# GpSimd's order at the start of an attention + MoE kernel: first value casts ahead of the band loads, last pair's keys and queries behind the first band table

## The chip, the cores and the metric

The kernel runs on one core of a Trainium2 chip. The time is in device microseconds; before the change it is 389.29 us, the median of 8 runs (388.36 to 390.95).

## What is computed

```python
# attention with a relative position bias; q, k, v: (8, 8, 576, 64)
scores = q @ k.T / 8 + bias_table[bucket(|i - j|)]   # one table column per head
attn   = exp(scores - max) / (sum + 1e-9)
x      = (attn @ v), heads side by side              # (4608, 512)
# act_snake layer
h   = x @ w_in                                       # w_in (512, 2048)
s   = sin(alpha * h)
g   = h + s * s / (alpha + 1e-9)
out = g @ w_out                                      # w_out (2048, 512)
```

The bucket of a distance is constant from a certain distance on. The kernel therefore multiplies exp(scores) by exp(bias - bias of the far bucket), and only in a band of 384 columns around the diagonal; outside it the factor is 1.

## The kernel before

The outer loop runs over the 8 batches. Within a batch the heads are taken in 4 pairs. For each pair TensorE makes scores for four key chunks of 128 keys (one half of the array per head), then a corner product `"t"` for the last 64 keys of both heads, then a last one for the last 64 queries (`plan_qk`, line 648). ScalarE takes the exponential of each (line 742), VectorE multiplies the band (lines 767 and 750, from the tables `m2r` and `mhr`), TensorE multiplies by the values (`plan_av`, line 779), VectorE divides by the sums (lines 839 and 840), and the result is turned into `xT`, the input of the MoE layer.

Keys and queries must be transposed (head dimension on partitions). For batches 0 and 1 TensorE does it: `plan_tr` (line 568) issues 12 transposes per pair and side (line 591), and a copy at line 564 brings them to `kT` or `qT`. Batch 0's first pair comes by SP's queue; the other three are loaded by GpSimd's queue into `nat1`, which shares its memory with a `u` buffer and is shown as `u` in the profile. For pairs 2 and 3 the last 64 keys are copied to `kt` by SP's queue (line 387). From batch 2 on the keys and queries are staged in DRAM and transposed by DMA.

The values of batch 0 come by SP's queue in fp32 (lines 501 and 504) into memory that later holds `w_out`, and GpSimd casts them to fp16: four chunks (line 418) and two halves for the last keys (line 421).

The band tables come from the small bias table: it is loaded by ScalarE's queue (`tabN`, `tabL`), a difference (line 511), an exponential (line 512), a matmul with a constant (line 529), a copy (line 530), a write to DRAM (`e_dram`, line 531). Then GpSimd loads shifted views of that row: `m2r` for heads 0 and 1, `mhr` in two loads, and `m2r` for heads 2 to 7 (lines 466 and 473). GpSimd's instructions run in the order in which they are written: a cast or a load that waits holds back all behind it, the loads of the weights and of batch 1's data too.

From `plan_qk` on, the order of instructions on TensorE, ScalarE and VectorE comes from a planner that runs when the kernel is built (`Plan.run`, line 109). Each task has an estimated length, dependences, a priority and an earliest due time. At each step the planner takes the task that could start first on its engine, and among those within 0.02 us of it the one of the lowest priority number. The engines then follow that order on the chip; the planned times themselves are not used there, only the semaphores are. Where TensorE would stand idle for more than 0.5 planned us before 30, the planner puts in a filler matmul on zeros (`warm`, line 454). Things that the planner can't see, such as loads, stand in constants of due times: `T_PAIR` (keys and queries of pairs 1, 2 and 3), `T_M2` (band multiplies of pair 0, and of the others), `T_MH` (the same for `mhr`), `T_V` (value products of batch 0 and of batch 1).

Of the kernel before, what the change touches and what calls it, by code (L numbers as in the profile page):

```python
# [180 lines left out]
T_FREE = {"PE": 6.8, "ACT": 7.5, "DVE": 7.75}  # L181
T_KT0 = 6.7
T_QT0 = 7.75
T_PAIR = ((6.8, 7.5), (10.0, 12.0), (10.0, 12.0))
T_M2 = (16.8, 20.0)
T_MH = (18.0, 18.0)
T_V = (18.5, 50.0)
T_TR1 = (36.0, 38.5)
T_KQ2 = 50.0
D_SPLIT = 3.5  # L190
# [23 lines left out]
def kernel(  # L214
# [12 lines left out]
    T, H, S, D = q.shape  # L227
# [81 lines left out]
    nat1 = ubs[2][0:SN, 0 : 2 * (H - 2) * SI * D].rearrange("s (kq h x) -> s kq h x", kq=2, h=H - 2)  # L309
# [105 lines left out]
    def cast_v(t, eng, cs):  # L415
        for c in cs:
            if c < 4:
                eng.tensor_copy(out=vs[t][:, c, :, 0:D], in_=vst[t][:, c])
                continue
            z = c - 4  # L420
            eng.tensor_copy(
                out=vhs[t][64 * z : 64 * z + 64, :, VC * z : VC * z + D],
                in_=vhst[t][64 * z : 64 * z + 64],
            )

    def load_nat(dst, h0, h1, src, eng):

        eng.dma_start(out=dst, in_=src[h0:h1].rearrange("h (p i) d -> p h (i d)", i=SI))

    def load_w_in16(js):  # L430
        src = moe_w_in.rearrange("(j p) ff -> p j ff", p=128)
        for j in js:
            nc.gpsimd.dma_start(out=w_in16[:, j, :], in_=src[:, j, :])
# [8 lines left out]
    def clear(eng, i):  # L442
        eng.memset(kts[i][0:64, :, 64:128], 0.0)
        eng.memset(kts[i][64:128, :, 0:64], 0.0)
        eng.memset(vhs[i][0:64, :, VC : 2 * VC], 0.0)
        eng.memset(vhs[i][64:128, :, 0:VC], 0.0)
        eng.memset(vhs[i][0:64, :, D : D + 1], 1.0)
        eng.memset(vhs[i][64:128, :, VC + D : VC + D + 1], 1.0)
        eng.memset(vs[i][:, :, :, D : D + 1], 1.0)
# [14 lines left out]
    def load_m2r(eng, h0, h1):  # L464

        eng.dma_start(
            out=m2r[:, h0:h1],
            in_=bass.AP(tensor=e_dram, offset=EW * h0, ap=[[1, 128], [EW, h1 - h0], [1, XW]]),
        )

    def load_mhr(eng):
        for z in range(2):
            eng.dma_start(
                out=mhr[64 * z : 64 * z + 64],
                in_=bass.AP(tensor=e_dram, offset=EW * z + 192,
                            ap=[[1, 64], [2 * EW, NP], [1, 192]]),
            )

    P_ = nc.gpsimd
# [23 lines left out]
    for z in range(2):  # L503
        nc.sync.dma_start(out=vhst[0][64 * z : 64 * z + 64], in_=vq[z, 512:S])
    for kq, src in ((0, k), (1, q)):
        load_nat(nat1[:, kq, 2:6], 4, H, src[0], P_)

    nc.vector.memset(zz, 0.0)
    clear(nc.vector, 0)
# [6 lines left out]
    def turn0(kq):  # L516
        c = bank("moE").bitcast(F16)
        for i in range(SI):
            nc.tensor.transpose(
                out=c[:, i * SN : i * SN + SN], in_=natb[:, kq, i], identity=id_sb[0:SN, 0:SN]  # L520
            )
        nc.vector.tensor_copy(  # L522
            out=(qTs if kq else kTs)[0][:, 0, :].rearrange("d (p i) -> d p i", i=SI),
            in_=c[:, 0:S].rearrange("d (i p) -> d p i", i=SI),
        )
# [5 lines left out]
    nc.scalar.dma_start(out=e_dram.ap(), in_=e_sb)  # L531
    turn0(1)
    clear(P_, 1)
    load_m2r(P_, 0, 2)
    load_mhr(P_)
    cast_v(0, P_, (0, 1))
    load_m2r(P_, 2, H)
    load_w_in16((0,))
    cast_v(0, P_, (2, 3, 4, 5))
    load_w_in16((1, 2, 3))  # L540
    for kq, src in ((0, k), (1, q)):
        load_nat(nat2[:, kq], 0, H, src[1], P_)
# [185 lines left out]
    def plan_ex(t, y, sc, b, u, ub, m, gate, base, done, x0):  # L728
# [17 lines left out]
        if i == "t":  # L746

            def bh(e):
# [4 lines left out]
            done[(1, 4)] = plan.add({"DVE": 0.19}, bh, [x], base + 10,  # L753
                                     nb=0.0 if t else T_MH[p > 0], use=[ub])
            return x
        w = 0 if i < 4 else 1
        q0, n = QW[w]
        for cc in [i] if i < 4 else range(4):
# [5 lines left out]
            def bd(e, cc=cc, lo=lo, hi=hi):  # L764
# [7 lines left out]
            done[(w, cc)] = plan.add({"DVE": 0.1 + (hi - lo) / 960.0}, bd, [x], base + 10,  # L772
                                     nb=0.0 if t else T_M2[p > 0], use=[ub])
        return x
# [4 lines left out]
    def plan_av(t, p, w, u, ub, done):  # L779
# [15 lines left out]
        if split:  # L795

            def part(e):
                av.v = bank(ab.tag)
                for i, qc in enumerate(QC[w]):
                    for z in range(2):  # L800
                        for c in range(3):
# [3 lines left out]

            prev = [plan.add({"PE": 0.62}, part, us[:3], base + AV_PRI, nb=T_V[t], new=[ab],
                             use=[ub])]
        for i, qc in enumerate(QC[w]):
# [14 lines left out]
            if t == 0 and w == 1 and i == 0:  # L823
                needs = [done[(0, c)] for c in range(4)] + [done[(1, 4)]]
            prev = [plan.add({"PE": 0.12 if split else 0.31}, mm, needs + prev,
                             base + AV_PRI + i, nb=T_V[t] if t < 2 else 0.0,
                             new=[ab] if i == 0 and not split else [],
# [174 lines left out]
    for t in range(T):  # L1002
# [23 lines left out]
        for p in range(NP):  # L1026
            if t == 0 and p + 1 < NP:
                for kq in range(2):
                    tr[(0, p + 1, kq)] = plan_tr(0, p + 1, kq, 100 * (16 * p + 8), T_PAIR[p][kq])
            deps.append(pe_gate + (tr[(t, p, 0)][0] + tr[(t, p, 1)][0] if t < 2 else []))  # L1030
# [69 lines left out]
```

The softmax here doesn't subtract the row's maximum and nothing guards it: scores larger than these inputs give would overflow.

## Time and profile before

| | us |
|---|---|
| median of 8 runs | 389.29 |
| the profiled execution | 390.05 |
| its span, first to last instruction | 388.3 |
| TensorE (PE) busy | 373.5 (96%) |
| ScalarE (ACT) busy | 319.2 (82%) |
| VectorE (DVE) busy | 264.8 (68%) |
| GpSimd (POOL) busy | 82.7 (21%) |
| exponentials of batch 0, first start to last end | 10.61 to 32.93 |
| first sine of the MoE layer | 38.12 |
| first exponential of batch 1 | 56.65 |

In the views of the trace, PE stands for TensorE's matmuls, PEld for its weight loads, ACT for ScalarE, DVE for VectorE, POOL for GpSimd, SP for SyncE. L418 is line 418 of the kernel. A row of the view in order of time has the start, the length, the engine, the line, the operation, output and input, the count of instructions merged in the row and, in brackets, how long the engine was idle before it and what ended that. A length may reach into the next instruction, since instructions are pipelined. A DMA is said to land when its semaphore shows it complete; its time to landing is counted from the start of its issue.

### The profile page before, as it was taken

The page shows a single profiled execution, that of the slowest core. Times are in us where ns is not written, and L with a number is a line of the kernel's source. Part 1 is how long each engine was busy: PE and PEld are TensorE (multiplying, and loading weights), DVE is VectorE, ACT ScalarE, POOL GpSimd, SP SyncE. Part 2 cuts the span into 40 slices and gives each one's busy share as a digit, 9 for nine tenths or more (in the row PEclk, how much of TensorE's full clock was granted, in tenths as well). Part 3 has the DMA queues.
Part 4 walks back from the last instruction along what each step waited for, and adds up shares of the span by engine and source line. Part 5 has one row for each costly group of instructions (what it writes and reads, how often), then busy time and mean ns, then how long its engine had stood idle before and what let it go on. Part 6 is the DMA issues. An engine that isn't in the chain of part 4 may idle for free.

```text
span 388.3 us, 8540 instructions
## 1 busy us (share of the span) xinstructions
PE 373.5 (96%) x3398; PEld 186.6 (48%) x3398; DVE 264.8 (68%) x589; ACT 319.2 (82%) x449; POOL 82.7 (21%) x98
## 2 busy tenths in 40 slices
PE   5989979999999999999999999999999999999996
PEld 2456434555545644555445535543555444444443
DVE  3776986686887698679867977697668718429100
ACT  2896999999999999999999999999999728529210
POOL 6583835072540071006300400000000000000000
PEclk9999999999999999999999999999999999999999
DMA  9899999999999999959991938210021010020122
GB/s 174 180 201 214 176 191 172 149 166 150 170 147 157 189 120 142 182 62 75 146 179 47 71 35 209 61 31 29 29 60 31 29 65 16 30 81 0 56 81 81
DMA packets 151207, 42.55 MB, mean 110 GB/s; under 512 B 140216, under 2 KB 145680, under 8 KB 151168
## 3 DMA queue, kind: packets, MB, share of 16 engines
q0 software_dynamic: 89872, 19.04, 58.8%
q1 hardware_dynamic: 61136, 22.93, 31.8%
q8 instruction: 26, 0.43, 0.5%
q14 instruction: 13, 0.11, 0.1%
q10 hardware_dynamic: 160, 0.04, 0.1%
HBM read 37.73 MB, written 16.52 MB: 140 GB/s over the span
## 4 chain that ended last, share of the span: by engine, by line
PE 88%; ACT 6%; DVE 2%; issue 2%; DMA 1%; ACTq 0%; DVEq 0%
PE sc L452 41%; PE am L452 38%; PE ca L452 4%; PE cb L452 4%; ACT u L742 3%; DMA tabL<-in_bias_table_dram 1%; ACT s L920 1%; DVE g L934 1%; ACT sq L927 1%; PE cb L591 0%; DVE qT L564 0%; PE am L591 0%; DVE qT L522 0%; ACT kT L562 0%; ACT outs L562 0%
## 5 line engine op out<-in xcount | busy, mean ns | idle before, releaser
L742 ACT ACTIVATE u<-sc 128x1024 f16<-128x1024 f32 (+1 forms) x192 | 156.3, 898 | 8.6 <-PE sc L452 7.3
L452 PE MATMUL sc<-xT,w_in 128*128 128x512 f16 x576 | 133.4, 379 | 0.4 <-DVE g L934 0.4
L934 DVE SCALAR_TENSOR_TENSOR g<-sq,inv_a,sc 128x512 f16<-128x512 f16 x144 | 103.8, 745 | 26.1 <-PE am L452 21.4
L452 PE MATMUL am<-w_out,g 128*128 128x512 f16 (+1 forms) x464 | 117.3, 374 | 0.7 <-ACT outs L562 0.7
L920 ACT ACTIVATE s<-sc,alphaT 128x512 f16<-128x512 f32 x144 | 92.4, 680 | 6.5 <-PE sc L452 5.5
L767 DVE TENSOR_TENSOR u<-u,m2r 128x512 f16<-128x512 f16 (+2 forms) x160 | 67.8, 441 | 29.0 <-ACT u L742 27.5
L452 PEld LDWEIGHTS <-g 128*128 128x128 f16 x592 | 54.3, 98 | 66.2 <-issue 14.0
L452 PEld LDWEIGHTS <-w_in 128*128 128x128 f16 x576 | 54.6, 98 | 63.0 <-issue 0.8
L452 PEld LDWEIGHTS <-u 128*128 128x128 f16 x1440 | 54.7, 97 | 16.0 <-issue 4.6
L452 PE MATMUL am<-v,u 128*128 128x65 f16 x1216 | 52.4, 193 | 0.0
L452 PE MATMUL sc<-qT,kT 64*128 64x64 f16 (+1 forms) x512 | 48.3, 295 | 4.1 <-ACT u L742 2.1
L927 ACT ACTIVATE sq<-s 128x512 f16<-128x512 f16 x76 | 47.4, 631 | 2.3 <-DVE g L934 0.5
L398 POOL DMA_DIRECT2D v<-in_v_dram x24 | 21.2, 894 | 109.7 <-PE am L452 107.7
L452 PE MATMUL am<-vh,u 128*128 128x130 f16 x152 | 33.4, 221 | 0.6 <-ACT u L742 0.3
L929 DVE TENSOR_TENSOR sq<-s 128x512 f16<-128x512 f16 x68 | 28.5, 419 | 6.5 <-ACT s L920 6.2
L452 PEld LDWEIGHTS <-kT 64*128 64x128 f16 x512 | 13.8, 95 | 31.8 <-issue 28.9
L840 DVE TENSOR_TENSOR xp<-am,rd 128x384 f16<-128x384 f32 (+1 forms) x56 | 27.5, 491 | 2.1
L839 DVE RECIPROCAL rd<-am 128x6 f32<-128x6 f32 (+1 forms) x60 | 11.2, 187 | 20.0 <-PE am L452 19.6
L562 ACT ACTIVATE outs<-am 128x512 f32<-128x512 f32 x7 | 4.2, 597 | 18.5 <-PE am L452 18.5
L564 DVE COPY outs<-am 128x512 f32<-128x512 f32 (+1 forms) x22 | 14.7, 668 | 3.9 <-PE am L452 3.7
L994 ACT ACT_TABLE_LOAD x13 | 16.7, 1283 | 0.2
L564 DVE COPY outs<-cb 128x384 f32<-128x384 f32 x1 | 0.6, 558 | 23.2 <-PE cb L452 23.2
(92 smaller groups left out, 181.0 us busy)
## 6 DMA issues: line engine op xcount, KB each, us to landing
out_dram<-outs SPq DMA_DIRECT2D x35, 256.0 KB, 2.0
staged_k<-in_k_dram POOLq DMA_DIRECT2D x6, 576.0 KB, 14.5
staged_q<-in_q_dram POOLq DMA_DIRECT2D x6, 576.0 KB, 19.4
v<-in_v_dram POOLq DMA_DIRECT2D x24, 128.0 KB, 8.8
w_in<-in_moe_w_in_dram POOLq DMA_DIRECT2D x4, 512.0 KB, 8.5
w_out<-in_moe_w_out_dram POOLq DMA_DIRECT2D x4, 512.0 KB, 17.3
xT<-xp SPq DMA_TRANSPOSE x72, 3.6
w_out<-in_v_dram SPq DMA_DIRECT2D x4, 256.0 KB, 8.9
```

What stands on the lines that cost most here:

```text
L398: nc.gpsimd.dma_start(out=vs[t % 2][:, c, :, 0:D], in_=vp[128 * c : 128 * c + 128],)
L452: nc.tensor.matmul(out=out, lhsT=lhsT, rhs=rhs, start=start, stop=stop)
L564: k_of(e).tensor_copy(out=o, in_=i)
L742: nc.scalar.activation(out=o, in_=x, func=AF.Exp, scale=0.125)
L767: nc.vector.tensor_tensor(out=io, in0=io, in1=m2[:, 2 * p : 2 * p + 2, x0 : x0 + hi - lo], op=ALU.mult,)
L839: nc.vector.reciprocal(out=r, in_=a[:, :, :, D])
L840: nc.vector.tensor_tensor(out=y.rearrange("p c (z d) -> p c z d", z=2), in0=a[:, :, :, 0:D], in1=r.unsqueeze(3).to_broadcast([128, nq, 2, ...
L920: nc.scalar.activation(out=s16.v, in_=h.v, func=AF.Sin, scale=alphaT[:, f : f + 1])
L927: nc.scalar.activation(out=sq.v, in_=s16.v, func=AF.Square)
L929: k_of(e).tensor_tensor(out=sq.v, in0=s16.v, in1=s16.v, op=ALU.mult)
L934: nc.vector.scalar_tensor_tensor(out=gcell[b].v[:, f, :], in0=sq.v, scalar=inv_a[:, f : f + 1], in1=h.v, op0=ALU.mult, op1=ALU.add,)
L994: nc.scalar.preload_act_table_set(name)
```

## The change

The loads of keys and queries of pairs 2 and 3 (one load each for `k` and `q`) are divided: pair 2's stay where they were, pair 3's are issued by GpSimd later, behind the `mhr` loads. The four casts of value chunks, which stood two between the band loads and two behind the first load of `w_in`, move up: chunks 0 and 1 ahead of the first band load, chunk 2 behind it, chunk 3 behind `mhr`. The two casts of the last keys' values stay. Due times of the planner are changed with it: pair 2's keys and queries earlier (9.5, 10.5), pair 3's later (16.5, 17.5), pair 0's band multiplies earlier (15.9) and the others' later (21.5), `mhr` at 17.8, batch 0's value products later (19.2).

```diff
-T_PAIR = ((6.8, 7.5), (10.0, 12.0), (10.0, 12.0))
-T_M2 = (16.8, 20.0)
-T_MH = (18.0, 18.0)
-T_V = (18.5, 50.0)
+T_PAIR = ((6.8, 7.5), (9.5, 10.5), (16.5, 17.5))
+T_M2 = (15.9, 21.5)
+T_MH = (17.8, 17.8)
+T_V = (19.2, 50.0)
...
     for kq, src in ((0, k), (1, q)):
-        load_nat(nat1[:, kq, 2:6], 4, H, src[0], P_)
+        load_nat(nat1[:, kq, 2:4], 4, 6, src[0], P_)
...
     clear(P_, 1)
+    cast_v(0, P_, (0, 1))
     load_m2r(P_, 0, 2)
+    cast_v(0, P_, (2,))
     load_mhr(P_)
-    cast_v(0, P_, (0, 1))
+    cast_v(0, P_, (3,))
+    for kq, src in ((0, k), (1, q)):
+        load_nat(nat1[:, kq, 4:6], 6, H, src[0], P_)
     load_m2r(P_, 2, H)
     load_w_in16((0,))
-    cast_v(0, P_, (2, 3, 4, 5))
+    cast_v(0, P_, (4, 5))
     load_w_in16((1, 2, 3))
```

## The prediction

> **What bounds the kernel now.** I read the page first (TensorE busy 96% of the span, the chain that ended last 88% TensorE), then the busy times of a few stretches, to see where TensorE is not full:
>
> ```profile
> core 0: us, PE busy (x) PEld busy (x) DVE busy (x) ACT busy (x) POOL busy (x), PEclk, DMA share, GB/s
> 0.00:10.60 10.60, 5.83 (x34) 2.50 (x34) 4.12 (x15) 2.08 (x3) 6.23 (x18) 1.00 0.96 177
> 10.60:33.00 22.40, 21.11 (x282) 11.58 (x283) 17.35 (x46) 20.52 (x25) 14.49 (x21) 1.00 0.98 192
> 33.00:38.10 5.10, 4.75 (x67) 3.21 (x67) 2.77 (x10) 2.37 (x4) 2.53 (x2) 1.00 1.31 222
> 38.10:56.65 18.55, 16.60 (x156) 7.60 (x155) 16.44 (x27) 18.05 (x31) 12.84 (x17) 1.00 1.69 184
> 75.00:100.00 25.00, 25.00 (x348) 14.30 (x347) 17.78 (x51) 23.74 (x32) 9.19 (x8) 1.00 1.89 162
> 200.00:300.00 100.00, 99.60 (x998) 51.03 (x995) 77.51 (x176) 95.89 (x133) 4.79 (x6) 1.00 0.39 67
> ```
>
> From 75 us on TensorE is full, so its remaining work fixes the end. Whatever moves the end of batch 0's attention (about 38 us) moves the end of the kernel by as much: the next stage, to 56.65, has ScalarE at 18.05 of 18.55. The change lies wholly ahead of 38 us. There I read the order in time of GpSimd, ScalarE and VectorE in turn:
>
> ```profile
> 13.64 0.73 POOL L466 DMA_DIRECT2D m2r<-e_dram  x1 [5.70 <-DMA e_dram<-e_sb]
> 14.37 1.26 POOL L473 DMA_DIRECT2D mhr<-e_dram  x2
> 15.62 1.18 POOL L418 CAST v<-w_out 128x512 f16<-128x512 f32 x2
> 16.73 0.84 POOL L466 DMA_DIRECT2D m2r<-e_dram  x1
> ```
>
> GpSimd idles 5.70 us for the bias table (7.94 to 13.64): this is the hole that the change fills.
>
> ```profile
> 14.90 0.65 ACT L742 ACTIVATE u<-sc 128x576 f16<-128x576 f32 x1 [0.19 <-PE sc L452]
> 15.85 8.05 ACT L742 ACTIVATE u<-sc 128x512 f16<-128x512 f32 x9 [0.30 <-PE sc L452]
> 24.39 3.98 ACT L742 ACTIVATE u<-sc 128x1024 f16<-128x1024 f32 x5 [0.48 <-PE sc L452]
> ```
>
> ScalarE's exponentials run from 10.61 to 32.93 with these gaps (0.19, 0.30, 0.48) and two later ones (0.30, 0.15): 1.42 us in all is what a better order on TensorE could give.
>
> ```profile
> 18.25 2.89 DVE L767 TENSOR_TENSOR u<-u,m2r 128x512 f16<-128x512 f16 x4 [0.59 <-DMA m2r<-e_dram]
> 23.45 0.20 DVE L839 RECIPROCAL rd<-am 128x6 f32<-128x6 f32 x1 [1.84 <-PE am L452]
> 24.70 0.41 DVE L767 TENSOR_TENSOR u<-u,m2r 128x512 f16<-128x512 f16 x1
> 35.08 0.20 DVE L839 RECIPROCAL rd<-am 128x6 f32<-128x6 f32 x1 [0.52 <-PE am L452]
> ```
>
> VectorE waits 0.59 us for the first band table, then 1.84 us for pair 0's value product; from 23.45 to 34.56 it has next to no gap. So the first normalisation, that is the place of pair 0's value product on TensorE, sets when batch 0 ends, and the bias table does not.
>
> **The change part by part.** (The planner's due times run ahead of the chip: due 18.5 is met at 22.34 us, due 10 and 12 at 12.42 and 14.79.)
>
> *First casts into the wait.* Two casts, 0.59 us each by the row above. Chunk 0 landed at 9.3 us (issued 2.69, 6.6 to landing), chunk 1 at 13.3 (3.59, 9.7). Were chunk 1 as late again, its cast would end at 13.9 and the first table load, now behind it on GpSimd, would start 0.25 late. But half of the bytes of pairs 2 and 3 leave this stretch: their two loads landed at 11.7 and 13.7, the pair-1 load before them at 8.6, so 576 KB took 5.1 us and half should be through at about 11.2; chunk 1 then lands near 12. The table's own write took until 13.6 (issued 9.17); the quickest landing of any store in the trace is 1.6 us. So the table load starts between 12.6 (chunk 1 cast) and 13.9; I take 12.9. Worth on the path: 0, since it meets VectorE's 0.59 us wait, which is followed by the idle 1.84. If that cover went, VectorE would gain at most the 0.59.
>
> *Later casts.* At 18.12 to 20.82 GpSimd casts while VectorE multiplies; those multiplies take 0.805, 0.957 and 0.745 us against 0.415 and 0.548 after 24.7. Casting two chunks earlier frees up to 1.0 us of VectorE (the excess of these three), again ahead of its idle 1.84: 0.
>
> *Pair 3's transposes leave 13.58 to 17.6.* Each set of 12 costs 0.62 us on the chain, and queries of pair 2 take one of the freed places. So the product before the 0.19 gap is as late as now, while that before the 0.30 gap comes 0.62 earlier: −0.30. Bounds 0 (something else fills the place) and −0.49 (both gaps).
>
> *Pair 3's loads.* GpSimd now has table 0.73, cast 0.59, second table (2 issues) 1.26, cast 0.59, then keys and queries at 0.70 each (the row of the 144 KB loads): keys issued at 12.9+3.17 = 16.1, queries at 16.8. Landing: by the table loads just ahead 3.9 to 4.5 us, so keys at 20.0 to 20.6, queries 20.7 to 21.3; the far bound is the 6.2 us of the second table load, 22.3 and 23.0. (Chunk 2, cast in between at 13.6, landed at 14.6 and chunk 3, cast at 15.5, at 15.4; chunk 2 no earlier than now would hold GpSimd, and so the keys, back 1.0.) Where are they used? Due 16.5 puts the keys behind pair 1's corner product (19.89 now), in the place of the filler matmul at 20.37. TensorE works in order, and behind them is pair 1's last product, whose exponential starts at 21.37 now and at 21.07 after the −0.30. That product needs about 0.45 and the transposes 0.62: keys are wanted by 20.0. At the middle landing, 20.3, TensorE and then ScalarE wait 0.3; queries are a slot later and land in it. +0.3, bounds 0 and +2.3. The Trainium skill (DMA: Bandwidth & Descriptors, Anatomy of one DMA — SWDGE) fits a GpSimd-issued transfer as about 2.0 us plus bytes over 436 GB/s; by it the keys would land 2.3 us after issue and the wait would be 0. The trace's 96 KB loads took 3.9 and 4.2 us from the start of issue, so I keep 0.3.
>
> *The second band table and the values.* The table's second load moves behind the two loads (+1.4), with two casts ahead of it as now, and starts 0.7 earlier: issued near 17.5 instead of 16.73. With its 6.2 us it lands at 23.7 instead of 22.9, or at 25.2 if the queue is full and the 288 KB ahead of it take 1.5 (192 GB/s in the second row above). It is first used at 24.70: hidden by 1.0, or exposed by 0.5. But the due times matter more. Pair 0's value product goes from due 18.5 to 19.2, so it may fall behind one more score product, and each of those waits for an exponential of 1.02 us; pair 1's band multiplies go from due 20.0 to 21.5. The first normalisation (23.45) then shifts by 0 to 1.0; against it, the product in front removes ScalarE's 0.48 gap, which does not help a full VectorE. I take +0.6, bounds 0 and +1.5 (the 1.0 and the exposed table).
>
> *What else is passed.* SP: the two small copies of pair 3's key tail follow its keys, at some 21.5 us plus 4.1 to 7.2 to landing (such copies now), wanted at 30.77. GpSimd: the same instructions follow; the last first-weight load lands at 32.8 and is used at 35.48, batch 1's keys 35.9 and 39.31, the last second-weight quarter 65.1 and 66.33. A queue 1 us later stays under all three: 0.
>
> Sum: −0.30 + 0.3 + 0.6 = +0.6 us. The profiled execution took 390.05 (span 388.3 plus 1.75 around it) and would take 390.65; it stands 0.76 above the median of the eight runs, so against the median 389.29 the forecast is 389.9.
>
> **Rivals.**
> 1. *Late keys (slower).* Pair 3's keys land at 21.2 us or later, the product behind them waits over 1.2 us, ScalarE starves. For it: landings were 6.2 us and more wherever two queues were busy. Against: the queue is at 0.35 to 0.88 busy between 14 and 19 us. Chunk 2 at its old time is enough. Price 1.2 to 2.3 in place of 0.3, with the rest: 390.8 to 391.9.
> 2. *TensorE stays slow (slower).* Up to about 21 us a 512-column filler takes 0.61 and 12 transposes 0.69; later 0.38 (25.70) and 0.45 (39.31), although the granted clock reads 1.00 throughout. The fast rate came only after four fillers in a row (17.33 to 20.37). Pair 3's transposes take the last one's place and may bring a wait. If the fast rate then comes after pair 0's value product (1.61 us, 22.34 to 23.95), that product takes 1.6 longer and VectorE's first normalisation 1.0 to 1.6: 390.7 to 391.5. The Trainium skill (TensorE: Matmul & The Clock Gate, Part 1) says that about 3.4 us of sustained matmuls bring the full clock; by it TensorE, busy since 8.45, would be fast before the fillers and this rival would cost 0. The trace shows over 12 us of busy slow matmuls.
> 3. *The gaps go (faster).* Keys land in time, pair 0's value product is no later, the gaps 0.30 and 0.48 close and VectorE follows (−0.8), up to all 1.42 of gaps and the 0.59 us wait (−2.0): 387.3 to 388.5. For it: VectorE has idle 1.84 us to absorb pair 3's two copies. Against: VectorE is full from 23.45 on.
>
> **How the numbers follow.** Forecast 0.38 (its own range 389.0 to 390.9), rival 1 0.17, rival 2 0.20, rival 3 0.25. Faster or slower means by over 0.3%, 1.2 us, about what a measurement tells from no change. Faster: 0.18 of rival 3 and 0.01 of the forecast. Slower: 0.11 of the forecast, 0.14 and 0.16 of the two slow rivals. The rest, 0.40, is within. The range, 387.8 to 391.9, leaves some 0.2 out: the best third of rival 3 and what lies beyond the prices of rivals 1 and 2.
>
> **What would show it.** Right: GpSimd's wait ahead of the first table load cut to under 1 us (behind the cast of chunk 1); no gap ahead of the exponential at 15.5; a TensorE or ScalarE gap of a few tenths near 20.5; VectorE's first reciprocal near 24.0 and the first sine half a microsecond after 38.1. Rival 1: a wait of the transposes at line 591 on a load, over 1 us. Rival 2: value products of 0.3 to 0.6 us for 9 matmuls near 23. I am wrong if the first reciprocal comes before 23.45, or if the order of the stages after 38 us itself changes TensorE's idle time there.

## The result and the profile after

The changed kernel takes 391.35 us (median of 17 runs, 390.43 to 391.99) against 389.57 us before (46 runs), a ratio of 1.0047 with a 95% interval of 1.0036 to 1.0058: slower by some 1.8 us. The profiled execution took 391.24 us with a span of 389.5.

In order of time, GpSimd (columns: start, length, engine, line, operation, in brackets the idle time before it and what ended it):

```profile
8.92 0.61 POOL L418 CAST v<-w_out 128x512 f16<-128x512 f32 x1 [0.94 <-DMA w_out<-in_v_dram]
11.17 0.62 POOL L418 CAST v<-w_out 128x512 f16<-128x512 f32 x1 [1.64 <-DMA w_out<-in_v_dram]
13.23 0.73 POOL L466 DMA_DIRECT2D m2r<-e_dram  x1 [1.45 <-DMA e_dram<-e_sb]
13.96 0.62 POOL L418 CAST v<-w_out 128x512 f16<-128x512 f32 x1
14.52 1.25 POOL L473 DMA_DIRECT2D mhr<-e_dram  x2
15.76 0.62 POOL L418 CAST v<-w_out 128x512 f16<-128x512 f32 x1
16.32 0.65 POOL L428 DMA_DIRECT2D u<-in_k_dram  x1
16.96 0.64 POOL L428 DMA_DIRECT2D u<-in_q_dram  x1
```

The change does what it says: the wait for the bias table holds two casts and shrinks from 5.70 to 1.45 us. Pair 3's keys are issued at 16.32 and land 3.2 us later, at 19.55. TensorE wanted them a microsecond before:

```profile
17.89 0.69 PE L452 MATMUL sc<-qT,kt 128*128 128x288 f16 x2
19.60 0.45 PE L595 MATMUL cb<-id_sb,u 96*64 96x96 f16 x12 [1.02 <-DMA u<-in_k_dram]
19.98 0.51 PE L452 MATMUL sc<-qT,kT 64*128 64x64 f16 x10
20.41 0.45 PE L595 MATMUL am<-id_sb,u 96*64 96x96 f16 x12
20.96 0.39 PE L452 MATMUL sc<-qT,kT 64*128 64x512 f16 x2
21.87 0.45 PE L452 MATMUL sc<-qT,kT 64*128 64x512 f16 x2 [0.52 <-ACT u L746]
22.26 0.29 PE L452 MATMUL am<-vh,u 128*128 128x130 f16 x1
...
25.11 0.56 PE L452 MATMUL sc<-qT,kT 64*128 64x512 f16 x2
```

The transposes (line 595 now) wait 1.02 us on the load, and the score product behind them waits too. Then the clock falls (busy time by stretch, PEclk is the granted clock):

```profile
core 0: us, PE busy (x) PEld busy (x) DVE busy (x) ACT busy (x) POOL busy (x), PEclk, DMA share, GB/s
18.00:19.00 1.00, 0.58 (x3) 0.05 (x1) 0.91 (x3) 1.00 (x2) 1.00 (x3) 1.00 0.94 132
19.00:20.00 1.00, 0.40 (x14) 0.34 (x16) 0.48 (x2) 0.27 (x1) 0.94 (x4) 1.00 1.21 204
20.00:21.00 1.00, 0.90 (x27) 0.62 (x25) 0.86 (x2) 0.69 (x2) 1.00 (x3) 1.00 1.02 143
21.00:22.00 1.00, 0.48 (x4) 0.15 (x3) 0.66 (x1) 1.00 (x2) 1.00 (x2) 1.00 0.87 246
22.00:23.00 1.00, 1.00 (x14) 0.75 (x13) 0.00 (x0) 1.00 (x2) 1.00 (x2) 0.54 1.10 225
23.00:24.00 1.00, 1.00 (x20) 1.00 (x19) 0.00 (x0) 0.65 (x1) 0.99 (x2) 0.50 0.92 155
24.00:25.00 1.00, 1.00 (x20) 1.00 (x17) 0.75 (x2) 0.00 (x0) 0.28 (x1) 0.50 1.04 201
25.00:26.00 1.00, 1.00 (x11) 0.47 (x9) 0.75 (x3) 0.29 (x1) 0.62 (x1) 0.76 1.11 214
```

From about 22.1 to 25.5 us TensorE runs at half clock. The whole of pair 0's value product lies in this stretch and takes 2.85 us (22.26 to 25.11). In the kernel before it takes 1.61, from the first to the second of these rows:

```profile
22.34 0.23 PE L452 MATMUL am<-vh,u 128*128 128x130 f16 x1
...
23.95 0.60 PE L452 MATMUL sc<-qT,kT 64*128 64x512 f16 x4
```

In the changed kernel ScalarE and VectorE show both losses:

```profile
20.31 3.35 ACT L746 ACTIVATE u<-sc 128x512 f16<-128x512 f32 x4 [1.04 <-PE sc L452]
25.71 3.98 ACT L746 ACTIVATE u<-sc 128x1024 f16<-128x1024 f32 x5 [2.06 <-PE sc L452]
...
24.12 0.20 DVE L843 RECIPROCAL rd<-am 128x6 f32<-128x6 f32 x1 [2.46 <-PE am L452]
25.77 0.41 DVE L771 TENSOR_TENSOR u<-u,m2r 128x512 f16<-128x512 f16 x1
```

ScalarE's gap of 1.04 is the late keys, that of 2.06 (0.48 before) the slow value product. One thing hides part of this when the two profiles are laid side by side: the first exponential starts at 9.14 us here and at 10.61 before, because the bias table landed 4.2 us after its issue and not 5.7. That is no effect of the change. The same instruction took 4.4 to 5.5 us in seven other profiles below, with the loads of pairs 2 and 3 divided or not. So I compare from the first exponential to the first sine of the MoE layer: 27.51 us before, 29.81 after, 2.3 us more. (Four profiles with the order of the kernel before on TensorE give 27.04 to 27.66.) The next stage, to batch 1's first exponential, is 18.53 and 18.29 us. This stretch tells where time is lost; how much is lost at the end is told by the runs, since what follows the first sine varies too: the time of the profiled execution less that of its first sine is 351.6 to 353.4 us in the twelve profiles.

### The profile page after: what moved, and what is told of

It is laid out like the page before. It is cut to its first block, busy times and chain, and to the rows that moved or that the text cites. A ratio compares the mean times of both kernels' runs of the same rounds, so it can differ in the third digit from the quotient of the medians.

```text
span 389.5 us, 8539 instructions
## 1 busy us (share of the span) xinstructions
PE 374.9 (96%) x3396; PEld 187.8 (48%) x3396; DVE 263.9 (68%) x588; ACT 319.2 (82%) x450; POOL 83.1 (21%) x100
## 4 chain that ended last, share of the span: by engine, by line
PE 89%; ACT 4%; DMA 3%; issue 1%; DVE 1%; POOL 1%; ACTq 0%; DVEq 0%
PE sc L452 42%; PE am L452 38%; PE ca L452 4%; PE cb L452 3%; ACT u L746 3%; DMA e_dram<-e_sb 1%; DMA tabL<-in_bias_table_dram 1%; DMA u<-in_k_dram 1%; PE cb L595 0%; ACT s L924 0%; ACT L998 0%; POOL mhr L473 0%; PE am L595 0%; POOL v L418 0%; DVE g L938 0%
## 5 line engine op out<-in xcount | busy, mean ns | idle before, releaser
L771 DVE TENSOR_TENSOR u<-u,m2r 128x512 f16<-128x512 f16 (+2 forms) x160 | 66.5, 433 | 31.9 <-ACT u L746 27.5
L452 PEld LDWEIGHTS <-u 128*128 128x128 f16 x1440 | 56.6, 99 | 15.9 <-issue 4.4
L452 PE MATMUL am<-v,u 128*128 128x65 f16 x1216 | 53.7, 195 | 0.0
```

Of the source, the lines that this page charges most:

```text
L452: nc.tensor.matmul(out=out, lhsT=lhsT, rhs=rhs, start=start, stop=stop)
L771: nc.vector.tensor_tensor(out=io, in0=io, in1=m2[:, 2 * p : 2 * p + 2, x0 : x0 + hi - lo], op=ALU.mult,)
```

## The experiments

Each theory is told in the expectations. The ratio is to runs of the kernel before that were taken along with it; the times (us) are from one profiled execution of each kernel.

| kernel | ratio, 95% interval | first exponential | first sine | between |
|---|---|---|---|---|
| before | 1 | 10.61 | 38.12 | 27.51 |
| the change | 1.0047 (1.0036 to 1.0058) | 9.14 | 38.95 | 29.81 |
| the change, again | 1.0040 (1.0024 to 1.0055) | 10.50 | 40.34 | 29.84 |
| pair 3's loads in the wait | 1.0000 (0.9986 to 1.0015) | 10.39 | 37.74 | 27.35 |
| due times alone | 1.0013 (0.9996 to 1.0030) | 9.36 | 38.57 | 29.21 |
| casts alone | 1.0004 (0.9993 to 1.0016) | 9.62 | 36.66 | 27.04 |
| fillers in the wait | 1.0027 (1.0016 to 1.0038) | 9.38 | 37.86 | 28.48 |
| pair 3 due later | 1.0077 (1.0054 to 1.0100) | 9.31 | 39.26 | 29.95 |
| bias table first | 0.9982 (0.9965 to 0.9998) | 8.75 | 36.41 | 27.66 |
| start freed of the bias table | 0.9964 (0.9947 to 0.9982) | 8.35 | 35.69 | 27.34 |
| fillers at batch 1's start, on before | 0.9992 (0.9976 to 1.0009) | 9.52 | 37.08 | 27.56 |
| the same, on the start freed | 0.9956 (0.9940 to 0.9972) | 8.36 | 35.69 | 27.33 |

**Pair 3's loads in GpSimd's wait.**

```diff
     clear(P_, 1)
+    for kq, src in ((0, k), (1, q)):
+        load_nat(nat1[:, kq, 4:6], 6, H, src[0], P_)
     cast_v(0, P_, (0, 1))
...
     cast_v(0, P_, (3,))
-    for kq, src in ((0, k), (1, q)):
-        load_nat(nat1[:, kq, 4:6], 6, H, src[0], P_)
     load_m2r(P_, 2, H)
```

> The changed kernel with one move: pair 3's two loads are issued by GpSimd in its wait for the bias table, ahead of the first two casts, and not behind mhr. The order on TensorE, ScalarE and VectorE is that of the changed kernel. Theory A (late keys): in the changed kernel TensorE waits 1.02 us for pair 3's keys (landed at 19.55), ScalarE then idles 1.04 and, after a stretch at half clock, 2.06 us; here the keys land by 14 us, the wait is gone and so is most of both gaps: 2 to 3 us under the changed kernel, ratio to the kernel before 0.992 to 0.998. Theory B (the planner's new order costs the time, the wait is hidden): the ratio stays at 1.003 to 1.006 although the wait is gone. Theory C (early bytes): the start of the exponentials, 9.14 us in the changed kernel and 10.61 before, comes from fewer bytes in front of the bias table's loads; it stays at about 9.1 here, since these loads are issued only after the bias table has landed.

Measured: 1.0000 (0.9986 to 1.0015). The whole loss is gone, with every instruction of TensorE, ScalarE and VectorE in the changed kernel's order. The loads go out at 7.99 and 8.62 and nothing waits for them:

```profile
7.99 0.64 POOL L428 DMA_DIRECT2D u<-in_k_dram  x1
...
14.68 0.72 POOL L466 DMA_DIRECT2D m2r<-e_dram  x1 [2.02 <-DMA e_dram<-e_sb]
...
16.08 7.83 ACT L746 ACTIVATE u<-sc 128x1024 f16<-128x1024 f32 x9 [0.21 <-PE sc L452]
24.50 3.98 ACT L746 ACTIVATE u<-sc 128x1024 f16<-128x1024 f32 x5 [0.58 <-PE sc L452]
...
23.57 0.20 DVE L843 RECIPROCAL rd<-am 128x6 f32<-128x6 f32 x1 [1.28 <-PE am L452]
```

ScalarE works through from 16.08, the value product runs at full clock, and the first reciprocal comes 13.18 us after the first exponential (12.84 before, 14.98 in the changed kernel). Theory A holds for the cause. Its size was overrated: I expected 0.992 to 0.998, and got no better than before. The order itself brings no gain. Theory C falls: the exponentials started at 10.39 with the same early bytes as in the changed kernel's profile. The band table went out at 14.68, later than in either kernel, at no cost.

**The due times alone.**

```diff
-T_PAIR = ((6.8, 7.5), (10.0, 12.0), (10.0, 12.0))
-T_M2 = (16.8, 20.0)
-T_MH = (18.0, 18.0)
-T_V = (18.5, 50.0)
+T_PAIR = ((6.8, 7.5), (9.5, 10.5), (16.5, 17.5))
+T_M2 = (15.9, 21.5)
+T_MH = (17.8, 17.8)
+T_V = (19.2, 50.0)
```

> The kernel before with the changed due times alone; loads and casts stand where they stood. Theory A: no load is late, pair 3's keys have landed at 11.7 us and are used at about 20; no wait of the transposes, ratio 0.998 to 1.002. Theory B: the order alone costs it, ratio 1.003 to 1.006. Theory C: exponentials start at 10.6 as before.

Measured: 1.0013 (0.9996 to 1.0030), which decides for neither number alone, but is under what theory B needs for the 1.0047. "No wait of the transposes" was wrong: pair 2's queries are now due earlier and are loaded with pair 3's, 576 KB together, so they land only at 13.3 us:

```profile
13.38 0.69 PE L591 MATMUL cb<-id_sb,u 96*64 96x96 f16 x12 [0.66 <-DMA u<-in_q_dram]
```

Its profile has gaps of 0.46 and 0.91 us on ScalarE for that. The order needs the divided load of pair 2. What remains after dividing it is the run above: nothing.

The same profile shows one thing more. Pair 3's transposes (19.77 and 21.14) waited for no load here, and yet TensorE was still slow: 0.69 us for 12 transposes, and 0.29 for the value product's first matmul. It became fast only near 23.9, within the value product, and ScalarE's gap behind it is 0.98 in place of 0.58 in the run above:

```profile
22.93 0.29 PE L452 MATMUL am<-vh,u 128*128 128x130 f16 x1
...
25.33 3.99 ACT L742 ACTIVATE u<-sc 128x1024 f16<-128x1024 f32 x5 [0.98 <-PE sc L452]
```

So a late load of pair 3 is not the only way to a slow value product.

**The casts alone.**

```diff
     clear(P_, 1)
+    cast_v(0, P_, (0, 1))
     load_m2r(P_, 0, 2)
+    cast_v(0, P_, (2,))
     load_mhr(P_)
-    cast_v(0, P_, (0, 1))
+    cast_v(0, P_, (3,))
     load_m2r(P_, 2, H)
     load_w_in16((0,))
-    cast_v(0, P_, (2, 3, 4, 5))
+    cast_v(0, P_, (4, 5))
```

> The kernel before with the four casts alone moved up (two ahead of the first band load, one behind it, one behind mhr); pairs 2 and 3 are loaded together as before and the due times are the old ones, so the order on TensorE is the old one. Theory A: chunk 1 lands at 13.3 as before, its cast pushes the first band load from 13.64 to about 13.9, VectorE's first band multiply comes 0.3 later in front of an idle 1.84 us; ratio 0.999 to 1.001. If the casts themselves cost (a rival): ratio over 1.003. Theory C: exponentials start at 10.6.

Measured: 1.0004 (0.9993 to 1.0016): the casts cost and bring nothing that these runs can tell from zero. The exponentials started at 9.62 with undivided loads, against theory C once more.

**Fillers in the wait.** Four matmuls on zeros run while TensorE waits for pair 3's keys.

```diff
-            c.v = bank("moE").bitcast(F16)
+            x0 = bank("moE")
+            if (t, p, kq) == (0, 3, 0):
+                for _ in range(4):
+                    full(x0, zz[:, 0:128], zz, True, True)
+            c.v = x0.bitcast(F16)
```

> The changed kernel with four filler matmuls on zeros put ahead of the transposes of pair 3's keys, so that TensorE is busy in most of the time in which it waits for them. Theory A with a clock part: the keys land as late as before and the gap of 1.04 us ahead of pair 1's last exponential stays, but the granted clock does not fall to 0.5 between 22 and 25.5 us and the gap of 2.06 us shrinks to under 1: 1 to 1.5 us under the changed kernel, ratio 1.000 to 1.003. If the half clock is no cause of the lost time: the ratio stays at 1.004 to 1.006.

Measured: 1.0027 (1.0016 to 1.0038). As expected, one loss stays and the other goes:

```profile
15.60 0.65 POOL L428 DMA_DIRECT2D u<-in_k_dram  x1
...
18.62 1.42 PE L452 MATMUL cb<-zz 128*128 128x512 f16 x4
19.98 0.45 PE L599 MATMUL cb<-id_sb,u 96*64 96x96 f16 x12
...
20.69 3.35 ACT L750 ACTIVATE u<-sc 128x512 f16<-128x512 f32 x4 [1.17 <-PE sc L452]
24.61 3.99 ACT L750 ACTIVATE u<-sc 128x1024 f16<-128x1024 f32 x5 [0.58 <-PE sc L452]
```

The gap of 1.04 is 1.17 here, that of 2.06 is 0.58, and the value product takes 1.61 us again (22.57 to 24.18). The fillers change no load and no order of the others, but they hold the transposes too: the keys, issued at 15.60, landed 3.7 us later, at 19.3, while the fillers ran until 19.98, and TensorE has no wait on the load in this profile. Without the fillers the wait would have been some 0.5 us (the product ahead ended at 18.83). So, by the middle values, of the loss of 0.40 to 0.47% some 0.13 to 0.20%, 0.5 to 0.8 us, was the slow clock or more, and 0.27%, 1.05 us, the wait or less. The intervals overlap, so these shares are estimates; that the slow value product cost time, the two gaps show.

**Pair 3 due later**, so that its transposes stand where the load has landed.

```diff
-T_PAIR = ((6.8, 7.5), (9.5, 10.5), (16.5, 17.5))
+T_PAIR = ((6.8, 7.5), (9.5, 10.5), (19.0, 20.0))
```

> The changed kernel with one constant moved: pair 3's keys and queries are due at 19.0 and 20.0 and not at 16.5 and 17.5. Loads and casts are as in the changed kernel, so the keys land as late; their transposes stand behind pair 2's third score product, some 4 us later on TensorE, with two more fillers ahead of them. If the loss is the wait at the place where the transposes stood: no wait on the load, no fall of the granted clock near 22 us, ratio to the kernel before 0.998 to 1.002. If the later loads cost in another way (the second band table or the weights behind them): the ratio stays at 1.003 to 1.006.

Measured: 1.0077 (1.0054 to 1.0100): slower still, and by neither of the two ways. The wait on the load is gone and the value product is fast (1.61 us, 21.99 to 23.60), but the queries' copy now stands deep in VectorE's full stretch:

```profile
28.78 0.42 DVE L844 TENSOR_TENSOR xn<-ca,rd 128x256 f16<-128x256 f32 x1
29.13 0.41 DVE L771 TENSOR_TENSOR u<-u,m2r 128x512 f16<-128x512 f16 x1
29.46 0.75 DVE L568 COPY qT<-am 128x576 f16<-128x576 f16 x1
...
29.10 0.49 ACT L566 ACTIVATE xT<-am 128x384 f16<-128x384 f16 x1 [2.65 <-PE am L881]
31.05 4.81 ACT L746 ACTIVATE u<-sc 128x1024 f16<-128x1024 f32 x6 [1.14 <-PE sc L452]
```

The queries' transposes were done at 24.3, the copy ran at 29.46, and ScalarE, out of scores, idled 2.65 and 1.14 us (and 1.33 ahead of 24.39). In this order the transposes have a window that opens when the load lands and closes when VectorE fills up.

**The change again**, for a second profile.

> The changed kernel once more, unaltered, for a second profile. In the profiles so far the first exponential starts anywhere from 9.1 to 10.6 us, with the landing of the bias table. If an early start is what makes pair 3's keys late (their landing hangs on the queue and not on the start): with a start near 9.2 the wait of the transposes is near 1 us as in the first profile, with a start near 10.5 it is under 0.3. Ratio 1.003 to 1.006.

Measured: 1.0040 (1.0024 to 1.0055), first exponential at 10.50. The wait followed the start, as expected, but not to under 0.3:

```profile
20.42 0.69 PE L595 MATMUL cb<-id_sb,u 96*64 96x96 f16 x12 [0.42 <-DMA u<-in_k_dram]
21.80 0.69 PE L595 MATMUL am<-id_sb,u 96*64 96x96 f16 x12
23.59 0.29 PE L452 MATMUL am<-vh,u 128*128 128x130 f16 x1
...
27.10 3.98 ACT L746 ACTIVATE u<-sc 128x1024 f16<-128x1024 f32 x5 [2.09 <-PE sc L452]
25.45 0.20 DVE L843 RECIPROCAL rd<-am 128x6 f32<-128x6 f32 x1 [2.17 <-PE am L452]
```

The wait was 0.42 us. TensorE had not become fast yet (0.69 us for 12 transposes) and stayed slow through pair 0's value product, which took the same 2.86 us (23.59 to 26.45). From first exponential to first sine it is 29.84, as in the first profile. In these two profiles the later start goes with a shorter wait, and not with a shorter sum.

**Bias table first**, on the kernel before.

```diff
-    nc.scalar.dma_start(out=phi_sb, in_=phi_h.ap())
     nc.scalar.dma_start(out=tabN, in_=bias_table)
...
+    nc.scalar.dma_start(out=phi_sb, in_=phi_h.ap())
     nc.sync.dma_start(out=alphaN, in_=moe_alpha.rearrange("(f p) -> f p", p=128))
```

> The kernel before with one swap on ScalarE's queue: the two loads of the bias table are issued ahead of the constant's, so some 0.45 us earlier. The bias table holds the first keys' copy on VectorE and so the start of the exponentials (10.61 us when it landed at 7.39, 9.1 to 9.6 when it landed near 6). If this start carries through to the end: the table lands 0.5 to 1.5 us earlier, first exponential at 9.0 to 9.8, ratio 0.997 to 0.999. If it doesn't carry through (a later stage waits for loads that don't come earlier): 0.9995 to 1.001.

Measured: 0.9982 (0.9965 to 0.9998), first exponential at 8.75: 0.7 us less by the ratio, for a start 0.4 to 1.9 us earlier than in the profiles of the old issue order. That some of the start carries through is likely, since the interval lies just under 1; how much is not shown.

**Start freed of the bias table**, on the kernel with pair 3's loads in the wait.

```diff
-    nc.scalar.dma_start(out=phi_sb, in_=phi_h.ap())
     nc.scalar.dma_start(out=tabN, in_=bias_table)
...
+    nc.scalar.dma_start(out=phi_sb, in_=phi_h.ap())
     nc.sync.dma_start(out=alphaN, in_=moe_alpha.rearrange("(f p) -> f p", p=128))
...
-    nc.vector.tensor_tensor(out=tabN, in0=tabN, in1=tabL, op=ALU.subtract)
-    nc.scalar.activation(out=tabE, in_=tabN, func=AF.Exp)
     warm(WARM0)
     cast0(1, P_)
+    nc.gpsimd.tensor_tensor(out=tabN, in0=tabN, in1=tabL, op=ALU.subtract)
+    nc.scalar.activation(out=tabE, in_=tabN, func=AF.Exp)
...
     turn0(0)
+    turn0(1)
...
-    turn0(1)
     clear(P_, 1)
```

> The kernel with pair 3's loads in GpSimd's wait, with the bias table's loads first, its subtraction on GpSimd instead of VectorE, and the first queries' transposes ahead of the bias matmul on TensorE, so that neither the first keys' nor the first queries' copy on VectorE waits for the bias table. If the start carries through: first exponential at 8.3 to 9.3 us in place of 10.4, ratio to the kernel before 0.994 to 0.998. If the stages behind it wait for other loads or for VectorE: exponentials start early and the time stays at 0.999 to 1.001.

Measured: 0.9964 (0.9947 to 0.9982), 388.12 us, 1.4 us under the kernel before by the ratio: the version that beats both kernels. It joins several edits; pair 3's loads in the wait alone gave 1.0000 and the bias table first 0.9982, the rest was not tried by itself. The first keys' copy on VectorE ran at 5.53 (7.57 before), the first exponential at 8.35:

```profile
8.35 2.88 ACT L746 ACTIVATE u<-sc 128x1024 f16<-128x1024 f32 x3 [0.59 <-PE sc L452]
```

**Fillers at batch 1's start**, 12 matmuls on zeros where TensorE idles between 54 and 58 us, on the kernel before and on the version above.

```diff
                 for (p, i), sc in zip(g, scs):
+                    if t == 1 and gi <= 1:
+                        fz = new_ps("am1")
+                        for _ in range(3):
+                            full(fz, zz[:, 0:128], zz, True, True)
```

> The kernel before with three filler matmuls on zeros ahead of each of batch 1's first four score products (12 in all, some 0.22 us each), where TensorE idles 0.3 to 1.1 us at a time between 54 and 58 us. In seven of the ten profiles so far the granted clock falls to 0.5 for 3 to 7 us there, in the one of the kernel before it doesn't. If that stretch costs time in most runs: no fall of the clock between 54 and 62 us, ratio 0.997 to 0.999. If the slow stretch is covered by ScalarE's exponentials: 0.9995 to 1.001, or above if the fillers push a score product back.

> The same twelve fillers in the kernel whose first copies no longer wait for the bias table (386.4 us span, 3 us at half clock near 56 to 59). If the slow stretch costs time: ratio to the kernel before 0.993 to 0.996, 0.5 to 1 us under the version without them. If it doesn't: 0.996 to 0.998.

Measured: 0.9992 (0.9976 to 1.0009) and 0.9956 (0.9940 to 0.9972). In both profiles the granted clock stays at 1.00 between 54 and 62 us, and two score products take 0.39 us there. Against the kernels without fillers the time can't be told apart (0.9956 beside 0.9964), so whether that slow stretch costs anything stays open. One sign says that it may: casts alone and the bias table first, whose profiles have half clock for some 6.8 us there, take 353.3 and 353.2 us from the first sine to the end, against 351.9 in the kernel before, whose profile has none. Pair 3 due later takes 353.4 without such a stretch.

## Why the prediction was right or wrong

The sign of the likeliest case was right and its size too small: +0.6 us was forecast, 1.8 measured. The time lies inside the range, but in the price of rivals 1 and 2 and not in the forecast's own. "Slower by over 0.3%", which came, had a chance of 0.41 in all.

- *First casts into the wait*, 0: right in its worth; the casts alone measure 1.0004. Chunk 1 was cast at 11.17 (taken: near 12), the table load started at 13.23 (taken: 12.9). GpSimd's wait ahead of it did not fall under 1 us, as the signs had it: it was 1.45, since the table's write took 5.2 us from its issue at 7.71.
- *Pair 3's transposes leave 13.58 to 17.6*, −0.30: too much. The gap of 0.30 closed, but one of 0.21 opened one exponential later (at 14.80 in the changed kernel, and in the others with its order).
- *Pair 3's loads*, +0.3: this is the step that failed, and not by the landing. The keys were issued at 16.32 (16.1 in the prediction) and landed after 3.2 and 3.7 us (3.9 to 4.5 taken). With the first exponential at 10.50, near the 10.61 from which the prediction worked, TensorE wanted them at 20.0, as predicted, and waited 0.42. With the start at 9.14 it wanted them at 18.58 and waited 1.02: the start was 1.36 earlier and the landing only 0.83 (19.55 against 20.38). So the moment of use was taken from one profile, while the start moves with the bias table by 1.5 us. What went wrong more was the cost behind the wait. The sum lets TensorE and ScalarE lose what the keys are late and counts nothing for a slow TensorE, which is left to rival 2; in both profiles the value product then took 2.85 us or more in place of 1.61, and ScalarE idled 2.06 and 2.09 us behind it (0.58 in the same order with the keys in time).
- The Trainium skill's fit for such a load (DMA: Bandwidth & Descriptors, Anatomy of one DMA — SWDGE) gives, as an estimate, 2.3 us from issue to landing. The trace shows 3.2 and 3.7; by the fit the wait would have been 0.1 us or nothing.
- *The second band table and the values*, +0.6: too much. With the same order and the loads early, the stretch to the first sine is 27.35 us, no longer than before's 27.51. The value product did move behind one more score product, and the first normalisation came 0.34 us later after the first exponential (13.18 against 12.84), but that did not reach the first sine. The second band table took 6.9 us to land in the changed kernel, at 24.5, and was first used at 25.77: hidden.
- *What else is passed*, 0: nothing in the runs speaks against it.
- The first normalisation came at 24.12, where the signs had it (near 24.0), but by luck: it started from an exponential 1.47 us earlier. In the second profile it came at 25.45.
- Rivals 1 and 2 were set beside each other as two cases, and both came at once. Rival 1's sign was there in the first profile (a wait of 1.02). Its ground, that landings took 6.2 us and more wherever two queues were busy, did not hold in the trace of the kernel before either: the first keys landed 3.4 us after their issue, the bias table's first load 3.7. Rival 2's place was right (pair 0's value product); its price of 1.6 us, a doubled product, was too much: the product took 1.24 longer (2.85 against 1.61), and less of that reached the end. (Its lower price, 390.7, should have been 390.9 by its own terms, 389.9 and 1.0.) In the second profile TensorE had not become fast, as rival 2 has it; in the first it had, and fell back.
- That the wait brings on the slow clock, by thinning TensorE's work, is argued: the fillers in the wait speak for it, and in every profile of this order without any wait on a load the value product was fast; but with the due times alone it was slow in part although pair 3's keys were in time, and only a load 6 us ahead was waited for. What is shown is that the loss goes when the keys come early.
- Rival 2's reading that the fast rate needs four fillers in a row came from one trace. With the casts alone, which have the same order on TensorE, the second filler was already fast, at 17.43.
- Rival 3's gaps: the 0.48 did not close even where the keys were in time (0.58); the order gives no gain.
- The premise that whatever moves the end of batch 0's attention moves the end of the kernel by as much is not borne out profile by profile: the casts alone reached the first sine 1.46 us before the kernel before, and the profiled execution took 0.09 less (389.96 against 390.05).

## What to carry to other kernels

A load that is moved behind others must be priced against the earliest moment at which an in-order engine may ask for it, over several executions, and not against one trace. Where the consumer's place in the order is fixed at build time, a late load stalls everything behind it; here a slow value product came with a wait of only 0.42 us, so the wait is not the whole price. What fixes TensorE's rate there is not shown. In this kernel GpSimd's hole was better filled with the issues of loads (0.64 us each) that someone waits for, ahead of casts for which nobody waits: 1.0000 against 1.0047.

## What the hardware showed that I had not expected

- The same 1 KB load of the bias table, issued at 1.7 us, landed 4.2, 4.4, 4.4, 4.4, 4.6, 4.7, 5.4, 5.5 and 5.7 us later in the nine profiles of kernels with it in the same place, and the whole start moved with it: the first exponential came from 9.14 to 10.61 us, in the same order.
- In the first profile of the change the clock fell to 0.5 at 22.1 us although TensorE had never idled more than 1.02 us at a stretch in the 4 us ahead of it; it was busy for 2.36 of them (0.58, 0.40, 0.90 and 0.48 in the four microseconds). The Trainium skill (TensorE: Matmul & The Clock Gate, Part 1) ties the fall to an idle window of some 3.4 us; here it fell after a thinly used stretch, in one profile.
- The granted clock reads 1.00 in stretches where TensorE is slow: in the second profile of the change, every microsecond from 19 to 27 reads 1.00, while the value product's matmuls take 0.29 us, as at a granted 0.50 in the first. In the version freed of the bias table the column reads 0.50 from 8 to 17 us, and its score products take the same 0.61 us for two as the earlier kernels' do under a reading of 1.00. The length of a known matmul is the surer sign.
- The moment at which TensorE becomes fast is not fixed by the order of its work. In four kernels with the same order there, the first score product or filler at the fast length starts at 22.02 (before), 17.43 (casts alone), 17.17 (bias table first) and 19.45 us (fillers at batch 1's start), which is 11.4, 7.8, 8.4 and 9.9 us after the first exponential.
